# An x ring of seven batches, and one x transfer issued 40 units earlier, in a two-problem attention kernel

## The chip, the cores and the metric

The kernel runs on one core of a Trainium2 chip. The metric is the device time of one execution in microseconds. Before the change the median of four runs is 1052.13 us (lowest 1049.18, highest 1055.1). The profile shown is of one further execution, whose own time is 1052.25 us; its span, from the first to the last profiled instruction, is 1050.5 us.

## The reference

Two independent problems, A and B, of the same shape. Each projects x to queries, attends over a given cache of keys and values, and projects the result; the two outputs are put side by side.

```
# per problem: B, Sq, D = 16, 144, 448;  H, Sk, Dh = 16, 512, 256;  all bfloat16
q = (x @ wq).reshape(B, Sq, H, Dh).transpose(0, 2, 1, 3)
scores = einsum("bhqd,bhkd->bhqk", q, k_cache) * Dh ** -0.5
p = softmax(scores, axis=-1)
o = einsum("bhqk,bhkd->bhqd", p, v_cache)
y = o.transpose(0, 2, 1, 3).reshape(B, Sq, H * Dh) @ wo
# result: concatenate([y_A, y_B], axis=-1), shape (16, 144, 896)
```

## The kernel before, in words

**Units and pairs.** A unit is one head of one batch of one problem: 2 x 16 x 16 = 512 units, numbered U, batch after batch (in the first 32 units two batches are interleaved). Units 0 to 47 take their keys from ordinary loads that TensorE transposes. From unit 48 on (`P0`) keys come from transposing DMAs, and units are handled in pairs, one even and one odd, where their softmax sums are concerned.

**Steps.** A loop over steps i emits the work of several units at different leads. In step i TensorE does the query projection Q of a later unit (L1132), the scores S of unit i+3 (L1163; i+2 before unit 48), the product PV of unit i (L1219), on even steps the row sum SM (L1235), and some matmuls of the output projection (L1335), as many as a rate table allows: one to three pieces of two matmuls in most steps. From unit 48 on most Q instructions do two batches of one head at once and are issued on every other step; for the first and last batches of a problem some do one.

**The softmax path of one unit.** ScalarE takes the exponential of the scores into pt_sb (L1173, two halves). GpSimd adds the four key chunks pairwise: a first add makes pp_sb (L1183), a second add makes one chunk of 128 rows in p2_sb (L1188; the profile writes it p_sb). VectorE adds the lower and upper 64 rows of that (t_halves, L1197, the half-add), into rows 0 to 63 of ps_sb for an even unit and 64 to 127 for an odd one. One matmul with a block matrix of ones then gives the row sums of both units of a pair (L1235). ScalarE makes reciprocals with a logarithm and exponentials (L1243, L1256), and VectorE multiplies PV by them into a ring that the output projection reads (t_evac_ot, L1271). VectorE also casts the queries out of PSUM (L1145 for one batch, L1146 for two) and keeps a running maximum and minimum of the row sums (t_check, L1286), reduced once in a while (L1292), from which one flag is made at the end.

In step i VectorE's program order is: query cast, output multiply of unit i-1, half-add of unit i+2, and on even steps the check of unit i. GpSimd's order is first add, second add, unit after unit.

**Waits.** A small recorder (`_Sched.add`) keeps, for each named buffer, who wrote and who reads it, and turns that into semaphore waits. An engine works in its program order, so an instruction that waits holds all those behind it on that engine. pp_sb and p2_sb have one buffer each, ps_sb has two, pt_sb has four.

**Transfers.** Nearly all DMAs are issued by SP, in one order. A planner makes that order (load_list and the loop behind it): every transfer has a due time (the modelled time of its first use), a step from which its destination is free, and an estimated duration; the planner goes through time, takes what is free soonest and, among these, what is due soonest. No order is made on the chip; SP waits on semaphores in the planned order. The kinds are: v, 512 KB for two units, in a ring of nine slots; k by transposing DMA, 16 units at a time (L1039), in a ring of 32 units; x by transposing DMA (t_load_x, L981 to L991) in a ring xt_sb of six batches, in eight groups; wq and wo, which are loaded for A at the start and again for B near the middle; and the output stores. A group of x that passes the end of the ring, the end of problem A or the end of problem B is split; the last batch of a problem needs three DMAs for its end. A load of x may be issued when the batches that held its slots have had their last query projection.

In what follows, x3 is the group of batches 14 to 17 (14 and 15 of A, 0 and 1 of B), and x4 is the group of batches 18 and 19, which are the third and fourth batch of B.

Of the kernel before, what the change touches and what calls it, by code (L numbers as in the profile page):

```python
# [752 lines left out]
def bass_concat_heads__mha_block_cached__gqa_block_cached__near_ridge_kernel(  # L753
# [23 lines left out]
    Bn, SQ, D = A_x.shape  # L777
    H, SK, DH = A_k_cache.shape[1], A_k_cache.shape[2], A_k_cache.shape[3]
# [3 lines left out]
    NT = NP * NU  # L782
# [4 lines left out]
    NWO = 2 * H  # L787
# [4 lines left out]

    LT = 4
    KW, KR = 16, 32
    NV, NX = 9, 6
    KG = 8
    NNAT = 24
    assert KR % KW == 0 and NU % KW == 0 and KW % KG == 0
# [1 line left out]
    assert X_GROUPS[-1][1] == NP * Bn and H == KW  # L800
    WQ_GROUPS = ((1, 2), (2, 4), (4, 8), (8, 12), (12, 16))
    WARM = 32
    NQT, NPT, NPS, NRI, NOST = 11, 4, 2, 2, 2
    RS = 3
    RC = RS * 128
    XR, X_AT = 48, {0: -4, 1: -2}
# [3 lines left out]

    P0 = NNAT * UV
    NCK = P0 + (NT - P0) // 2
    NRUN = max(n for n in range(1, 33) if NCK % n == 0)
    assert P0 % KG == 0
    HALF_WAVES = (48, 64)
    cuts = {P0} | set(range(P0 // KW * KW + KW, NT, KW)) | set(range(HALF_WAVES[0], HALF_WAVES[1], KG))
# [6 lines left out]
    with contextlib.ExitStack() as es:  # L823
        mem = contextlib.ExitStack()

        def sb(name, shape, dt):
            return mem.enter_context(nc.sbuf_tensor(name, shape, dt))

        def ps(name, shape, dt):
            return mem.enter_context(nc.psum_tensor(name, shape, dt))  # L830
# [8 lines left out]
        pt_sb = sb("pt_sb", [128, NPT, 4, SQ], BF16)  # L839
        ones = sb("ones", [128, 128], BF16)  # L840
        pp_sb = sb("pp_sb", [128, 2, SQ], F32)
        ps_sb = sb("ps_sb", [128, NPS, SQ], BF16)
        rinv_sb = sb("rinv_sb", [128, NRI, SQ], F32)
        p2_sb = sb("p2_sb", [128, SQ], F32)
        ln_sb = sb("ln_sb", [128, SQ], F32)
        run_sb = sb("run_sb", [128, 2, NRUN], BF16)
        runs_sb = sb("runs_sb", [128, 2, NCK // NRUN], F32)
        ost_sb = sb("ost_sb", [128, NOST, D], BF16)
        stat = sb("stat", [128, 4], F32)
        flag_sb = sb("flag_sb", [128, 4], I32)  # L850
        qp_ps = ps("qp_ps", [128, 2, 512], F32)
        s_ps = [ps("s_ps%d" % i, [128, 512], F32) for i in range(3)]
        ot_ps = [ps("ot_ps%d" % i, [128, 512], F32) for i in range(2)]
# [5 lines left out]
        S = _Sched()  # L859
# [19 lines left out]
        def unit(U):  # L879
            if U < 2 * H:  # L880
                return 0, U % 2, U // 2
            pr, r = divmod(U, NU)
            b, h = divmod(r, H)
            return pr, b, h

        def ls(U):

            return 2 if U < P0 else 3

        def lq(U):  # L890
            return ls(U) + 1
# [58 lines left out]
        def t_load_wo(pr, wg):  # L950
            c0 = wg * WOG
            w = wos[pr]

            def e(q):
                return q.dma_start(wo_sb[:, c0:c0 + WOG, :],
                                   w[c0 * 128:(c0 + WOG) * 128, :].rearrange("(c p) n -> p c n", p=128)).then_inc(
                    sems["wo%d" % wg], 16)
            over = [(("xn", g), 1) for g in range(NX) if pr == 0 and wg in x_rows(g)[2]]
            S.add(SP, e, writes=[(("wo", wg), pr)] + over, dma_sem="wo%d" % wg, name="wo%d.%d" % (pr, wg))

        def t_load_x(XG):
# [33 lines left out]

        def x_rows(g):
            n = SQ // XR
            c0 = NWO - (NX - g) * n
            return n, wo_sb[0:XR, c0:c0 + n, :], sorted(set(c // WOG for c in range(c0, c0 + n)))

        def t_load_xn(g):
            n, dst, _wgs = x_rows(g)

            def e(q):
                return q.dma_start(dst, xs[0][g].rearrange("(t p) d -> p t d", p=XR)).then_inc(sems["xn%d" % g], 16)
            S.add(SP, e, writes=[(("xn", g), 0)], dma_sem="xn%d" % g, name="xn%d" % g)
# [145 lines left out]
        def t_s(U):  # L1152
# [16 lines left out]
            for k in range(2):  # L1169
                bank = k if U < P0 else (2 * U + k) % 3  # L1170

                def x(a, k=k, bank=bank):
# [2 lines left out]
                S.add(ACT, x, reads=[(("sp", bank), 2 * U + k)], writes=[(("pt", psl), U)], banks=["s%d" % bank],  # L1175
                      name="ex%d.%d" % (U, k))

        def t_presum(U):
            psl = U % NPT
            sl = U % NPS  # L1180

            def e1(g):
                return g.tensor_tensor(pp_sb[:, :, :], pt_sb[:, psl, 0:2, :], pt_sb[:, psl, 2:4, :], op=ALU.add)  # L1183
            S.add(POOL, e1, reads=[(("pt", psl), U)], writes=[("pp", U)], name="pp%d" % U)
            dst, key = (ps_sb[:, sl, :], (("ps", sl), U)) if U < P0 else (p2_sb[:, :], ("p2", U))

            def e2(g):
                return g.tensor_tensor(dst, pp_sb[:, 0, :], pp_sb[:, 1, :], op=ALU.add)  # L1188
            S.add(POOL, e2, reads=[("pp", U)], writes=[key], name="ps%d" % U)

        def t_halves(U):

            sl = U // 2 % NPS
            p0 = U % 2 * 64

            def e(v):
                return v.tensor_tensor(ps_sb[p0:p0 + 64, sl, :], p2_sb[0:64, :], p2_sb[64:128, :], op=ALU.add)  # L1197

            S.add(DVE, e, reads=[("p2", U)], writes=[(("ps", sl), ("p", U // 2)), ("halves", U)], name="hv%d" % U)

        def ring_cols(pr, b):
            g0 = pr * RP + b * SQ
# [23 lines left out]
        def t_sum(U):  # L1226
            ob = U % 2
            if U < P0:
                rhs, keys = ps_sb[:, U % NPS, :], [("ones", 0), (("ps", U % NPS), U)]
            else:  # L1230
                sl = U // 2 % NPS
                rhs, keys = ps_sb[:, sl, :], [("ones", 1), (("ps", sl), ("p", U // 2))]

            def e(t):
                return t.matmul(ot_ps[ob][:, 2 * SQ:3 * SQ], lhsT=ones[:, :], rhs=rhs, start=True, stop=True)  # L1235
            S.add(PE, e, reads=keys, writes=[(("sum", ob), U)], banks=["ot%d" % ob], name="SM%d" % U)
# [43 lines left out]
        def t_check(U):  # L1280
            ob = U % 2
            n = U if U < P0 else P0 + (U - P0) // 2
            j = n % NRUN
            for k, op in ((0, ALU.max), (1, ALU.min)):
                def e(v, k=k, op=op):
                    return v.tensor_reduce(run_sb[:, k, j:j + 1], ot_ps[ob][:, 2 * SQ:3 * SQ], axis=AX.X, op=op)  # L1286
                S.add(DVE, e, reads=[(("sum", ob), U)], writes=[(("run", k), n // NRUN)], banks=["ot%d" % ob],
                      name="ck%d.%d" % (U, k))
            if j == NRUN - 1:
                for k, op in ((0, ALU.max), (1, ALU.min)):  # L1290
                    def e(v, k=k, op=op):
                        return v.tensor_reduce(runs_sb[:, k, n // NRUN:n // NRUN + 1], run_sb[:, k, :],  # L1292
                                               axis=AX.X, op=op)
# [75 lines left out]
        s_min = -LT  # L1369
# [4 lines left out]
        for r in range(NP * NCH):  # L1374
            pr, rl = divmod(r, NCH)
# [69 lines left out]
        def load_list():  # L1445
            made = []

            def load(use, free, took, fn, *args):
                made.append((at(use) - MARGIN, free, took, fn, args))

            for XG, (g0, g1) in enumerate(X_GROUPS):
                load(first_q[g0], (g1 - NX) * H - lq(NT) if g1 > NX else s_min, 1.3 + 0.55 * (g1 - g0), t_load_x, XG)
            for W, (u0, u1) in enumerate(WAVES):
                last = u1 - 1 - KR
                load(u0 - ls(u0), last - ls(last) + 1 if last >= 0 else s_min, K_FIX + 0.97 * (u1 - u0), t_load_k, W)
            for pr in range(NP):
                for h0, h1 in WQ_GROUPS if pr == 0 else [(h, h + 4) for h in range(0, H, 4)]:
                    load(first_h[pr, h0], NU - H + h1 - lq(NU) if pr else s_min, 0.78 * (h1 - h0), t_load_wq, pr, h0, h1)
                for wg in range(NWG):
                    load(wo_use[pr, wg], wo_done[pr - 1, wg] + 1 if pr else s_min, 1.3, t_load_wo, pr, wg)  # L1460
            for g in X_AT:
                load(X_AT[g], s_min, 0.4, t_load_xn, g)
            for u in range(4):
                load(u - LT, s_min, 0.72, t_load_n, u // 2, u % 2)
            for G in range(2, NNAT):
                load(UV * G - LT, None, 1.44, t_load_n, G)
            for G in range(NT // UV):
                load(UV * G, None, 1.44, t_load_v, G)
# [46 lines left out]
        while i < NT or i in op_at or dma_plan or stores:  # L1515
# [138 lines left out]
```

## Time and profile before

| | |
|---|---|
| median of four runs | 1052.13 us |
| the profiled execution's own time | 1052.25 us |
| its span | 1050.5 us |
| granted TensorE clock, mean | 0.997 |
| TensorE busy | 1031.4 us (98%), 12432 matmuls |
| VectorE busy | 797.1 us (76%) |
| ScalarE busy | 794.0 us (76%) |
| GpSimd busy | 630.7 us (60%) |
| DMA, mean over the span | 280 GB/s |
| first add, L1183 | 512 x 742 ns |
| second add, L1188, from unit 48 on | 464 x 488 ns |
| half-add, L1197 | 464 x 520 ns |
| a k transfer of B, from issue to landing (median) | 25.3 us |
| an x transfer of B, from issue to landing (median) | 5.4 us |

How to read it. The span is cut into the busy time of engines; PE is TensorE's matmuls and PEld its weight loads, DVE is VectorE, ACT ScalarE, POOL GpSimd, SP the engine that issues the transfers. In a row of the page, `out<-in` names the tiles by the kernel's own names with buffer numbers left out; then come the shape, the count, the busy time, the mean of one in ns, the idle time of the engine just before, and what ended it. [...] The DMA share is the sum of the packets' durations over 16 engines and may be over 1, when packets of one engine overlap.

### The profile page before, as it was taken

How to read it: one execution, taken by the hardware profiler on the slowest of the kernel's cores; microseconds unless marked ns; L12 is line 12 of the kernel's file. 1: busy time of each engine (PE TensorE's matmuls, PEld its weight loads, DVE VectorE, ACT ScalarE, POOL GpSimd, SP SyncE). 2: the span in 40 equal slices, each digit the busy share in tenths (PEclk: the TensorE clock that was granted, in tenths of full speed). 3: DMA queues.
4: the chain of work that ended last, by engine and by line, in shares of the span. 5: the costliest groups of instructions: out<-in, count | busy, mean ns of one | idle time of the engine just before them, and what ended most of it. 6: DMA issues, size and time to landing. Idle time of an engine off the chain costs nothing.

```text
span 1050.5 us, 32573 instructions
## 1 busy us (share of the span) xinstructions
PE 1031.4 (98%) x12432; PEld 878.0 (84%) x12432; DVE 797.1 (76%) x2042; ACT 794.0 (76%) x2368; POOL 630.7 (60%) x1030
## 2 busy tenths in 40 slices
PE   8999999999999999999999899999999999999997
PEld 8999888888788888888887688888888888888885
DVE  5776787778777787787686668888787777788774
ACT  5877677778777787878766568787787777788785
POOL 3655556666566666666655456666666666666673
PEclk9999999999999999999999999999999999999999
DMA  9999999999999999999999999999999999999960
GB/s 319 363 331 331 291 263 247 281 283 291 292 297 300 272 278 251 298 278 302 255 299 328 269 291 288 292 272 296 269 265 273 298 281 296 270 282 286 285 226 13
DMA packets 590884, 294.11 MB, mean 280 GB/s; under 512 B 501440, under 2 KB 515904, under 8 KB 590720
## 3 DMA queue, kind: packets, MB, share of 16 engines
q1 hardware_dynamic: 590240, 291.72, 111.5%
q8 instruction: 100, 1.64, 0.6%
q14 instruction: 64, 0.52, 0.2%
q10 hardware_dynamic: 480, 0.23, 0.1%
HBM read 161.74 MB, written 4.13 MB: 158 GB/s over the span
## 4 chain that ended last, share of the span: by engine, by line
PE 89%; DMA 8%; SPq 2%; issue 0%; DVE 0%; ACT 0%; DVEq 0%; ACTq 0%
PE ot_ps L1219 23%; PE s_ps L1163 22%; PE qp_ps L1132 22%; PE op_ps L1335 18%; DMA kt_sb<-in_B_k_cache_dram 2%; DMA kt_sb<-in_A_k_cache_dram 2%; PE ot_ps L1235 2%; DMA wq_sb<-in_A_wq_dram 1%; DMA v_sb<-in_B_v_cache_dram 1%; PE qp_ps L1083 1%; PE s_ps L1083 1%; SPq L1053 1%; DMA wq_sb<-in_B_wq_dram 1%; PE qp_ps L1335 1%; DMA v_sb<-in_A_v_cache_dram 0%; SPq L981 0%
## 5 line engine op out<-in xcount | busy, mean ns | idle before, releaser
L1183 POOL TENSOR_TENSOR pp_sb<-pt_sb 128x288 f32<-128x288 bf16 x512 | 380.0, 742 | 305.8 <-ACT pt_sb L1173 291.2
L1173 ACT ACTIVATE pt_sb<-s_ps 128x288 bf16<-128x288 f32 x1024 | 364.5, 408 | 180.6 <-PE s_ps L1163 174.8
L1163 PE MATMUL s_ps<-qt_sb,kt_sb 128*128 128x144 bf16 x4096 | 340.3, 226 | 5.9 <-DMA kt_sb<-in_B_k_cache_dram 4.9
L1219 PE MATMUL ot_ps<-pt_sb,v_sb 128*128 128x144 bf16 x4096 | 340.2, 226 | 3.5 <-DMA v_sb<-in_B_v_cache_dram 1.9
L1163 PEld LDWEIGHTS s_ps<-qt_sb,kt_sb 128*128 128x128 bf16 x4096 | 288.3, 98 | 54.7 <-issue 5.3
L1256 ACT ACTIVATE rinv_sb<-ln_sb 64x144 f32<-64x144 f32 x928 | 298.2, 321 | 24.2
L1132 PE MATMUL qp_ps<-xt_sb,wq_sb 128*128 128x288 bf16 (+1 forms) x2368 | 300.1, 270 | 2.2 <-DMA wq_sb<-in_B_wq_dram 1.0
L1335 PE MATMUL op_ps<-wo_sb,ring 128*128 128x448 bf16 x1120 | 285.8, 353 | 0.0
L1188 POOL TENSOR_TENSOR p_sb<-pp_sb 128x144 f32<-128x144 f32 x464 | 226.7, 488 | 92.6 <-DVE ps_sb L1197 53.5
L1219 PEld LDWEIGHTS ot_ps<-pt_sb,v_sb 128*128 128x128 bf16 x4096 | 274.2, 98 | 4.6 <-DVE ps_sb L1197 4.1
L1132 PEld LDWEIGHTS qp_ps<-xt_sb,wq_sb 128*128 128x128 bf16 x2368 | 211.8, 98 | 77.0 <-issue 1.6
L1146 DVE CAST qt_sb<-qp_ps 128x576 bf16<-128x576 f32 x216 | 163.3, 756 | 139.1 <-PE qp_ps L1132 138.9
L1197 DVE TENSOR_TENSOR ps_sb<-p_sb 64x144 bf16<-64x144 f32 x464 | 241.4, 520 | 34.7 <-POOL p_sb L1188 15.7
L1271 DVE TENSOR_TENSOR ring<-ot_ps,rinv_sb 128x288 bf16<-128x288 f32 (+2 forms) x640 | 237.4, 387 | 19.1 <-ACT rinv_sb L1256 14.2
L1286 DVE TENSOR_REDUCE run_sb<-ot_ps 128x1 bf16<-128x144 f32 x560 | 144.9, 300 | 42.2 <-ACT rinv_sb L1243 26.3
L1335 PEld LDWEIGHTS op_ps<-wo_sb,ring 128*128 128x128 bf16 x1120 | 94.0, 98 | 20.7 <-issue 0.5
L1243 ACT ACTIVATE ln_sb<-ot_ps 128x144 f32<-128x144 f32 x232 | 67.7, 292 | 34.6 <-PE ot_ps L1235 28.0
L1235 PE MATMUL ot_ps<-ps_sb,ones 128*128 128x144 bf16 x280 | 63.4, 226 | 0.0
L1145 DVE CAST qt_sb<-qp_ps 128x288 bf16<-128x288 f32 x80 | 36.0, 450 | 4.4 <-PE qp_ps L1132 3.6
L1091 ACT ACTIVATE kt_sb<-qp_ps 128x512 bf16<-128x512 bf16 x48 | 29.0, 605 | 1.1 <-PE qp_ps L1083 1.1
L1235 PEld LDWEIGHTS ot_ps<-ps_sb,ones 128*128 128x128 bf16 x280 | 27.4, 98 | 1.1 <-DVE ps_sb L1197 1.1
L1188 POOL TENSOR_TENSOR ps_sb<-pp_sb 128x144 bf16<-128x144 f32 x48 | 23.4, 488 | 6.9 <-PE ot_ps L1235 0.3
(37 smaller groups left out, 163.7 us busy)
## 6 DMA issues: line engine op xcount, KB each, us to landing
v_sb<-in_A_v_cache_dram SPq DMA_DIRECT2D x128, 512.0 KB, 7.4
v_sb<-in_B_v_cache_dram SPq DMA_DIRECT2D x128, 512.0 KB, 7.2
v_sb<-in_A_k_cache_dram SPq DMA_DIRECT2D x22, 512.0 KB, 10.1
out_dram<-ost_sb SPq DMA_DIRECT2D x36, 112.0 KB, 6.4
wo_sb<-in_A_wo_dram SPq DMA_DIRECT2D x8, 448.0 KB, 7.9
wo_sb<-in_B_wo_dram SPq DMA_DIRECT2D x8, 448.0 KB, 8.3
wq_sb<-in_B_wq_dram SPq DMA_DIRECT2D x4, 768.0 KB, 9.4
wq_sb<-in_A_wq_dram SPq DMA_DIRECT2D x3, 768.0 KB, 9.3
```

What stands on the lines that cost most here:

```text
L1132: ins = t.matmul(acc, lhsT=wq_sb[:, kc, c0:c0 + 128], rhs=xt_sb[:, kc, xo:xe + 1:max(xe - xo, 1), :], start=(kc == 0), stop=(kc == 3))
L1146: return v.tensor_copy(qt_sb[:, a:b + 1:b - a, :, :], qp_ps[:, :, 0:2 * SQ].rearrange("p e (u q) -> p u e q", u=2))
L1163: ins = t.matmul(s_ps[bank][:, (c % 2) * SQ:(c % 2 + 1) * SQ], lhsT=kt_sb[:, 2 * c + dc, ko:ko + 128], rhs=qt_sb[:, qsl, dc, :], start=(dc ...
L1173: return a.activation(pt_sb[:, psl, 2 * k:2 * k + 2, :].rearrange("p b q -> p (b q)"), s_ps[bank][:, 0:2 * SQ], AF.Exp, scale=DH ** -0.5)
L1183: return g.tensor_tensor(pp_sb[:, :, :], pt_sb[:, psl, 0:2, :], pt_sb[:, psl, 2:4, :], op=ALU.add)
L1188: return g.tensor_tensor(dst, pp_sb[:, 0, :], pp_sb[:, 1, :], op=ALU.add)
L1197: return v.tensor_tensor(ps_sb[p0:p0 + 64, sl, :], p2_sb[0:64, :], p2_sb[64:128, :], op=ALU.add)
L1219: ins = t.matmul(ot_ps[ob][:, dc * SQ:(dc + 1) * SQ], lhsT=v_sb[:, vsl, j, c * DH + dc * 128:c * DH + (dc + 1) * 128], rhs=pt_sb[:, sl, c, ...
L1256: return a.activation(rinv_sb[p0:p0 + 64, sl, :], ln_sb[h0:h0 + 64, :], AF.Exp, scale=-1.0)
L1271: ins = v.tensor_tensor(ring[:, 2 * h:2 * h + 2, r0:r0 + q1 - q0], ot_ps[ob][:, 0:2 * SQ].rearrange("p (c q) -> p c q", c=2)[:, :, q0:q1], ...
L1286: return v.tensor_reduce(run_sb[:, k, j:j + 1], ot_ps[ob][:, 2 * SQ:3 * SQ], axis=AX.X, op=op)
L1335: ins = t.matmul(acc[0:m, 0:D], lhsT=ring[:, c, col0:col0 + m], rhs=wo_sb[:, c, :], start=(c == op_first), stop=(c == op_last))
```

## The change

The x ring xt_sb goes from six batches to seven (`NX`), and the due time of x4 is set 40 units earlier. The larger ring takes 1152 bytes more of each partition, and these come from other buffers:

- p2_sb is gone; the second add writes over the first half of pp_sb, from which the half-add reads.
- ps_sb has one buffer in place of two. Before unit 48 the odd units use a part of the second output staging buffer instead.
- The run of row-sum reductions is 20 long in place of 28, so there are 14 runs in place of 10, kept in bfloat16, and the flag shares a tile with other small values.
- The two batches of x that are loaded in natural order at the start lie in the last six columns of wo_sb in place of earlier ones.

With seven slots the places where x groups pass the ring's end are others (multiples of seven), and so are the splits of the groups and the pairs of batches whose order is turned in a double query projection. The order of instructions on TensorE, ScalarE and GpSimd is the same as before; on VectorE only the reductions of runs stand elsewhere. On SP's queue x3 and x4 stand earlier, x3 ahead of the k transfer for units 192 to 207 and x4 ahead of that for units 224 to 239, and three v transfers stand one place earlier, ahead of a k transfer each.

```diff
-    NV, NX = 9, 6
+    NV, NX = 9, 7
...
-    NQT, NPT, NPS, NRI, NOST = 11, 4, 2, 2, 2
+    NQT, NPT, NRI, NOST = 11, 4, 2, 2
...
-    NRUN = max(n for n in range(1, 33) if NCK % n == 0)
+    NRUN = max(n for n in range(1, 21) if NCK % n == 0)
...
-        ps_sb = sb("ps_sb", [128, NPS, SQ], BF16)
+        ps_sb = sb("ps_sb", [128, SQ], BF16)
         rinv_sb = sb("rinv_sb", [128, NRI, SQ], F32)
-        p2_sb = sb("p2_sb", [128, SQ], F32)
...
-        runs_sb = sb("runs_sb", [128, 2, NCK // NRUN], F32)
+        runs_sb = sb("runs_sb", [128, 2, NCK // NRUN], BF16)
         ost_sb = sb("ost_sb", [128, NOST, D], BF16)
-        stat = sb("stat", [128, 4], F32)
-        flag_sb = sb("flag_sb", [128, 4], I32)
+        stat = sb("stat", [128, 8], F32)
+        flag_sb = stat.bitcast(I32)[:, 4:8]
...
-            c0 = NWO - (NX - g) * n
+            c0 = NWO - (len(X_AT) - g) * n
...
+        def ps_natural(U):
+            if U % 2:
+                return ost_sb[:, 1, 0:SQ], (("ost", 1), ("ps", U))
+            return ps_sb[:, :], ("ps", U)
...
-            dst, key = (ps_sb[:, sl, :], (("ps", sl), U)) if U < P0 else (p2_sb[:, :], ("p2", U))
+            dst, key = ps_natural(U) if U < P0 else (pp_sb[:, 0, :], ("pp", ("p2", U)))
...
-                return v.tensor_tensor(ps_sb[p0:p0 + 64, sl, :], p2_sb[0:64, :], p2_sb[64:128, :], op=ALU.add)
-
-            S.add(DVE, e, reads=[("p2", U)], writes=[(("ps", sl), ("p", U // 2)), ("halves", U)], name="hv%d" % U)
+                return v.tensor_tensor(ps_sb[p0:p0 + 64, :], pp_sb[0:64, 0, :], pp_sb[64:128, 0, :], op=ALU.add)
+
+            S.add(DVE, e, reads=[("pp", ("p2", U))], writes=[("ps", ("p", U // 2)), ("halves", U)], name="hv%d" % U)
...
-                load(first_q[g0], (g1 - NX) * H - lq(NT) if g1 > NX else s_min, 1.3 + 0.55 * (g1 - g0), t_load_x, XG)
+                load(first_q[g0] - (40 if g0 == Bn + 2 else 0), (g1 - NX) * H - lq(NT) if g1 > NX else s_min, 1.3 + 0.55 * (g1 - g0), t_load_x, XG)
```

More of the change, by code (lines that the diff above doesn't have):

```diff
@@ L957, in e @@
                     sems["wo%d" % wg], 16)
-            over = [(("xn", g), 1) for g in range(NX) if pr == 0 and wg in x_rows(g)[2]]
+            over = [(("xn", g), 1) for g in X_AT if pr == 0 and wg in x_rows(g)[2]]
             S.add(SP, e, writes=[(("wo", wg), pr)] + over, dma_sem="wo%d" % wg, name="wo%d.%d" % (pr, wg))
@@ L1176, in t_s @@
                       name="ex%d.%d" % (U, k))
+        def ps_natural(U):
+            if U % 2:
+                return ost_sb[:, 1, 0:SQ], (("ost", 1), ("ps", U))
+            return ps_sb[:, :], ("ps", U)
         def t_presum(U):
             psl = U % NPT
-            sl = U % NPS
             def e1(g):
@@ L1191, in t_halves @@
         def t_halves(U):
-            sl = U // 2 % NPS
             p0 = U % 2 * 64
             def e(v):
-                return v.tensor_tensor(ps_sb[p0:p0 + 64, sl, :], p2_sb[0:64, :], p2_sb[64:128, :], op=ALU.add)
-            S.add(DVE, e, reads=[("p2", U)], writes=[(("ps", sl), ("p", U // 2)), ("halves", U)], name="hv%d" % U)
+                return v.tensor_tensor(ps_sb[p0:p0 + 64, :], pp_sb[0:64, 0, :], pp_sb[64:128, 0, :], op=ALU.add)
+            S.add(DVE, e, reads=[("pp", ("p2", U))], writes=[("ps", ("p", U // 2)), ("halves", U)], name="hv%d" % U)
         def ring_cols(pr, b):
@@ L1228, in t_sum @@
             if U < P0:
-                rhs, keys = ps_sb[:, U % NPS, :], [("ones", 0), (("ps", U % NPS), U)]
-            else:
-                sl = U // 2 % NPS
-                rhs, keys = ps_sb[:, sl, :], [("ones", 1), (("ps", sl), ("p", U // 2))]
+                rhs, key = ps_natural(U)
+                keys = [("ones", 0), key]
+            else:
+                rhs, keys = ps_sb[:, :], [("ones", 1), ("ps", ("p", U // 2))]
             def e(t):
```

## The prediction

> **What bounds the kernel now.** I read the page first: TensorE is busy 98% of the span, so a gain can only come out of its waits, and a loss must make a new one. Then the list of waits for TensorE alone (engine, tile and line, what it waited for: us in total, times, longest):
>
> ```profile
> PE s_ps L1163 <- DMA kt_sb<-in_B_k_cache_dram: 4.9, 1, 4.9
> PE ot_ps L1219 <- DMA v_sb<-in_B_v_cache_dram: 1.9, 2, 1.2
> PE ot_ps L1219 <- DMA v_sb<-in_A_v_cache_dram: 1.4, 1, 1.4
> ```
>
> The large waits are for transfers, none for VectorE or GpSimd. TensorE's timeline puts three of problem B's at 523.25 (0.96, wq), 563.28 (1.20, v) and 603.76 (4.89, k). Then the table by windows (us, busy time and count of PE, PEld, DVE, ACT, POOL; granted clock, DMA share, GB/s), around the x transfer that SP issued at 463.04, and around the longest wait:
>
> ```profile
> 460.00:467.00 7.00, 7.00 (x81) 5.80 (x79) 5.98 (x18) 5.00 (x16) 4.13 (x8) 1.00 1.05 392
> 468.00:470.00 2.00, 2.00 (x32) 1.85 (x30) 1.97 (x6) 1.76 (x7) 1.26 (x3) 1.00 1.39 74
> 471.00:472.50 1.50, 1.50 (x23) 1.40 (x22) 0.87 (x3) 0.94 (x3) 0.99 (x2) 1.00 1.14 36
> 600.00:620.00 20.00, 16.24 (x166) 13.27 (x167) 10.38 (x28) 10.39 (x31) 7.44 (x13) 0.91 1.19 297
> ```
>
> The DMA engines are a second bound: in windows of 20 us their share is over 1 from 20 to 1000 us, at some 390 GB/s on v and 290 on transposes, and each change of kind leaves a hole: 2 us at 74 GB/s before the x data, 1.5 us at 36 behind it. The last line adds a clock of 0.91 after the long wait: 0.09 x 20 = 1.8 us more lost.
>
> The diff also takes buffers away on the GpSimd-VectorE path, so I read that path in one pair of units, GpSimd's timeline, then VectorE's (start, duration, engine and line, idle before it):
>
> ```profile
> 699.62 0.73 POOL L1183 TENSOR_TENSOR pp_sb<-pt_sb 128x288 f32<-128x288 bf16 x1
> 700.59 0.49 POOL L1188 TENSOR_TENSOR p_sb<-pp_sb 128x144 f32<-128x144 f32 x1 [0.24 <-DVE ps_sb L1197]
> 701.22 0.78 POOL L1183 TENSOR_TENSOR pp_sb<-pt_sb 128x288 f32<-128x288 bf16 x1
> ```
>
> ```profile
> 701.11 0.30 DVE L1197 TENSOR_TENSOR ps_sb<-p_sb 64x144 bf16<-64x144 f32 x1
> 701.40 0.52 DVE L1286 TENSOR_REDUCE run_sb<-ot_ps 128x1 bf16<-128x144 f32 x2
> 702.38 0.76 DVE L1146 CAST qt_sb<-qp_ps 128x576 bf16<-128x576 f32 x1 [0.46 <-PE qp_ps L1132]
> 703.05 0.45 DVE L1271 TENSOR_TENSOR ring<-ot_ps,rinv_sb 128x288 bf16<-128x288 f32 x1
> 703.53 0.78 DVE L1197 TENSOR_TENSOR ps_sb<-p_sb 64x144 bf16<-64x144 f32 x1
> ```
>
> GpSimd's first add of the next unit (0.73) runs beside VectorE's half-add, and its second add waits for that. A half-add takes 0.30 with GpSimd idle, 0.78 beside its first add.
>
> **The change part by part: the new wait.** With p2_sb folded into pp_sb, the first add of unit U+1 waits for the half-add of U; before, only the second add did. Behind it on GpSimd stand only the second add and the next units; VectorE's next half-add waits for these, and behind that in VectorE's order stand the check (L1286), the q eviction (L1146) and the output eviction (L1271), for which S and PV of the following units wait. The loop from half-add to half-add: handoff 0.08 (699.74+0.77=700.51 to 700.59), first add 0.73, gap 0.14 (701.22+0.78 to the second add at 702.15, rounded down), second add 0.49, handoff 0.03, half-add.
>
> [...] Its mean in the page is 520 ns, its list by line reads 302/306/847 (least, median, most). [...] By the mean the loop is 0.08+0.73+0.14+0.49+0.03+0.52=1.99 us a unit. [...] every half-add costs 0.30: 1.77 us. [...] I take 1.77. It also frees VectorE of about 0.47 us a pair, which no TensorE wait needs.
>
> Most pairs hold one double q eviction. From the odd unit's half-add: 0.30, then 0.08+0.73+0.14+0.49+0.03 and the even half-add 0.30 (2.07), the check 0.52 from 0.01 before its end (2.58), the q eviction 0.76 (3.34), the output eviction 0.45 from 0.09 before that ends (3.70), 0.03, the next odd half-add: 3.73 us a pair. TensorE's row sums at 700.75 and 704.55 stand 3.80 apart, and over 620 to 1000 its 1568 score matmuls, 8 a unit, give 3.88 on average. So the wait hides, with 0.07 to spare in the tightest pairs and 0.15 on average. Where several tight pairs follow, or the q evictions are shorter and so faster paced, I let the trace's starts slip by the loop: 0.3 to 0.8 us of lateness near 382, 437, 460, 500 and 570, which the DMA waits at 523 to 604 swallow (7.05 us together), and 0.4 us in all near 720 and 973, on the path (bounds 0 and 0.8).
>
> The cover is gone in the last units. Two row sums one pair apart in TensorE's timeline:
>
> ```profile
> 1021.73 0.23 PE L1235 MATMUL ot_ps<-ps_sb,ones 128*128 128x144 bf16 x1
> 1021.79 0.54 PE L1335 MATMUL op_ps<-wo_sb,ring 128*128 128x448 bf16 x2
> ...
> 1025.05 0.23 PE L1235 MATMUL ot_ps<-ps_sb,ones 128*128 128x144 bf16 x1
> ```
>
> 3.32 us a pair there, against 2 x 1.77 = 3.54: 0.22 lost in each of the last 8 pairs, 1.76, less about 0.25 of margin that is used up first: +1.5 (bounds 0.5 and 2.5).
>
> The single ps_sb makes the even half-add wait for the row sum of the pair before: that ends at 700.75+0.23=700.98, the half-add starts at 701.11 now and 0.2 later after: nothing. Below unit 48 the odd unit's slot is ost_sb's second, which no output chunk uses so early: nothing. Four more pairs of run reductions (176 ns each, 1.4 us in all), a zeroing of 64x504 for 64x432 (418 ns, some 0.07 more) and the packed flag lie in VectorE's idle quarter: nothing; with no cover the reductions cost 1.4.
>
> **The change part by part: the transfers.** On SP's queue only this moves: x4 (second problem's batches 3 and 4; issue 3.96 at 463.04) goes ahead of the k transfer of 433.45; x3 (four DMAs at 400.39, 5.6) ahead of the k transfer of 370.53; and the v transfers for units 204, 220 and 252 go each ahead of the k transfer they followed. Splits of x at ring ends change (15 x DMAs before and after): x1 and x5 in two, x2 whole, x7 three for four.
>
> The two k transfers behind x start up to 5.6 and 4.0 later. They land at 391.50 and 455.30 and are first used at 403.99 and 465.23: 12.5 and 9.9 us to spare, so no wait. The k transfers of 406.06 and 467.06 can be issued 2.8 and 2.6 sooner, but issuing is not moving: v data queued before 463 still flows at 390 GB/s till 467.5. The same bytes and as many changes of kind lie before 604 in another order. What is really won is the hole around the four x DMAs at 401 to 409 (share 0.29, 1 GB/s from 404 to 406), which now falls under a v backlog. Nothing won is one bound; the other is x4's whole passage, 467.5 to 472.5, off the queue before 604: 4.5 of the 4.89 us and the 1.8 of the clock with it. I take 1.2, near the low end, since the share leaves little idle DMA time to win: -1.2. The v transfer behind x5 lands 1.4 us before its use; the split may cost it 0 to 0.5: +0.2.
>
> **Sum**, on the profiled execution (1052.25: span 1050.5 and 1.75 around it): 1052.25 + 1.5 + 0.4 + 0.2 - 1.2 = 1053.15. The median shown is 0.12 lower, so 1053.0.
>
> **The rivals.** (a) *The x transfer was hidden anyway and what it wins, the loop gives back* (my forecast): x4 lands 91 us ahead of its first use. 1053.0.
> (b) *Faster: x4's passage comes off the DMA-bound stretch whole.* For it: from 515.9 on SP issues to 604 without waiting for an engine, each transfer late by the one before it. Against: the DMA engines are as full where x4 goes. 1052.1 - 4.5 - 1.8 + 2.1 = 1047.9; with the waits at 523 and 563 gone as well, 1045.7. [...] The trace has this one wait to go by; I keep the 1.8.
> (c) *Slower: the half-add loop becomes the bound everywhere.* Place: handoff to the first add and VectorE's order behind it. It decides once a pair's loop is 0.15 longer than my 3.73. At 0.2 longer: 0.05 on 105 pairs from 604 on is 5.3, the last 8 pairs 1.6 more; earlier ones are swallowed: 1053.0 + 6.9 = 1059.9. For it: only 0.07 to spare in tight pairs, and a handoff read from a few rows. Against: every term is a repeated row.
> (d) *Slower: a k or v transfer pushed back by x misses its use*: 2 to 5 us, 1057.
>
> **How the numbers follow.** Chances: (a) 0.57, (b) 0.17, (c) 0.18, (d) 0.08. The runs before spread over 1049.18 to 1055.1, so 0.5% (5.3 us, below 1046.9 or above 1057.4) is about what a measurement can tell from no change. Faster by that needs (b) with the earlier waits gone too: 0.12. Slower: (c) and part of (d), with some of (a)'s spread: 0.28. Within: 0.60. The range holds (a), most of (b) and (c): 1046.5 to 1061.
>
> **What would show it.** Right: half-adds nearly all near 0.30; first adds released by the half-add instead of the exponential; row sums about 3.54 apart at the end, with TensorE waiting on the half-add there and nowhere for long; the wait near 604 still over 3 us. Wrong on (b) if that wait is under 1 us; wrong on (c) if row sums stand over 3.9 apart between 620 and 1000; wrong on (d) if a transfer of k before 500 us has a wait behind it.

## The result and the profile after

| | before | after |
|---|---|---|
| median of the runs | 1051.6 us (63 runs) | 1057.47 us (42 runs) |
| ratio, 95% interval | | 1.0048, [1.0038, 1.0059] |
| the profiled execution's own time | 1052.25 us | 1056.6 us |
| its span | 1050.5 us | 1054.8 us |
| VectorE busy | 797.1 us | 706.0 us |

The change costs 5.1 us (0.0048 x 1051.6; 4.0 to 6.2). The forecast, 1053.0, stood for a cost of 0.9. The measured time lies inside the range of 1046.5 to 1061, at the edge of the 0.5% that was called no change.

The page's rows of after for the first add, the second add and the half-add:

```profile
L1186 POOL TENSOR_TENSOR pp_sb<-pt_sb 128x288 f32<-128x288 bf16 x512 | 373.0, 729 | 374.8 <-DVE ps_sb L1199 246.1
L1191 POOL TENSOR_TENSOR pp_sb<-pp_sb 128x144 f32<-128x144 f32 x464 | 226.7, 489 | 36.4
L1199 DVE TENSOR_TENSOR ps_sb<-pp_sb 64x144 bf16<-64x144 f32 x464 | 141.2, 304 | 158.1 <-POOL pp_sb L1191 128.9
```

The half-add fell from 520 to 304 ns, and the first add now waits for it: 246.1 us of GpSimd's idle time are released by VectorE. That much is as forecast, and it costs nothing by itself. What costs is read from TensorE. Its list of waits in after:

```profile
PE s_ps L1162 <- DMA kt_sb<-in_B_k_cache_dram: 4.5, 1, 4.5
PE ot_ps L1221 <- DMA v_sb<-in_A_v_cache_dram: 3.9, 1, 3.9
PE s_ps L1082 <- DMA v_sb<-in_A_k_cache_dram: 1.7, 4, 0.7
PE ot_ps L1221 <- DMA v_sb<-in_B_v_cache_dram: 1.2, 1, 1.2
```

The long k wait near 604 is still there (4.9 before), and the v wait that was 1.4 is 3.9. TensorE's timeline puts them in place:

```profile
269.76 0.91 PE L1221 MATMUL ot_ps<-pt_sb,v_sb 128*128 128x144 bf16 x8 [3.91 <-DMA v_sb<-in_A_v_cache_dram]
503.13 0.67 PE L1162 MATMUL s_ps<-qt_sb,kt_sb 128*128 128x144 bf16 x8 [0.51 <-DVE qt_sb L1144]
606.54 1.12 PE L1162 MATMUL s_ps<-qt_sb,kt_sb 128*128 128x144 bf16 x8 [4.55 <-DMA kt_sb<-in_B_k_cache_dram]
```

The middle row is new: before the change no matmul between 425 and 510 us waited for VectorE. The table by windows of after (us, busy time and count of PE, PEld, DVE, ACT, POOL; granted clock, DMA share, GB/s):

```profile
260.00:280.00 20.00, 16.09 (x168) 12.87 (x166) 9.41 (x25) 10.72 (x33) 9.19 (x16) 0.91 1.08 321
...
600.00:620.00 20.00, 15.45 (x147) 11.98 (x145) 8.16 (x22) 9.11 (x27) 7.38 (x13) 0.83 1.17 307
```

Before, the clock was 1.00 in the first and 0.91 in the second. Half clock for 3.41 us is 1.7 us lost and takes 0.09 off a window of 20 us. Ahead of the last units before has one stretch of this length, from 603.50; after has one, from 270.02, and one of 6.83 us, from 604.52.

And the last units, row sums of two pairs, then GpSimd and VectorE beside them:

```profile
1028.55 0.23 PE L1237 MATMUL ot_ps<-ps_sb,ones 128*128 128x144 bf16 x1
1032.17 0.23 PE L1237 MATMUL ot_ps<-ps_sb,ones 128*128 128x144 bf16 x1
```

```profile
1026.83 0.73 POOL L1186 TENSOR_TENSOR pp_sb<-pt_sb 128x288 f32<-128x288 bf16 x1 [0.55 <-ACT pt_sb L1172]
1027.64 0.49 POOL L1191 TENSOR_TENSOR pp_sb<-pp_sb 128x144 f32<-128x144 f32 x1
1028.61 0.73 POOL L1186 TENSOR_TENSOR pp_sb<-pt_sb 128x288 f32<-128x288 bf16 x1 [0.48 <-DVE ps_sb L1199]
1029.41 0.49 POOL L1191 TENSOR_TENSOR pp_sb<-pp_sb 128x144 f32<-128x144 f32 x1
```

```profile
1026.39 0.30 DVE L1199 TENSOR_TENSOR ps_sb<-pp_sb 64x144 bf16<-64x144 f32 x1 [1.05 <-PE s_ps L1162]
...
1028.16 0.31 DVE L1199 TENSOR_TENSOR ps_sb<-pp_sb 64x144 bf16<-64x144 f32 x1 [0.31 <-POOL pp_sb L1191]
...
1030.01 0.30 DVE L1199 TENSOR_TENSOR ps_sb<-pp_sb 64x144 bf16<-64x144 f32 x1 [1.05 <-PE s_ps L1162]
```

A pair takes 3.62 us where it took 3.32. The three engines' rows show one closed loop: half-add, first add, second add, half-add. From an even half-add to the odd one it takes 1.77 us. Back again it takes 1.85: the second add ends at 1029.90, and the even half-add starts 0.11 later; the odd one starts 0.03 after its second add (1028.13 to 1028.16). The even one has two semaphores to wait for since the half-sums have one buffer: GpSimd's, for the second add, and TensorE's, for the row sum of the pair before. That row sum was done at 1028.78, so the TensorE named in the row was not what it waited for; the second wait is there all the same. All half-adds of this trace for which VectorE stood idle show it: from the end of the second add to their start, the even ones take 104 ns (median of 122, 102 to 105) and the odd ones 34 ns (125, 33 to 35). On TensorE the delay shows at the weight loads: between 1005 and 1038 us those of L1162 stand idle for 3.7 us for the q cast (L1144), which is queued on VectorE behind the half-add.

**Where the time went, unit by unit.** I take the time between two row sums, subtract TensorE's DMA waits in between, and subtract the same of before. Units 494 to 508: 23.23 us before, 25.37 after, no DMA wait in either: +2.14 (0.31 a pair over 7 pairs). Units 200 to 240, where query casts are single: 427.14 to 500.55 before, 429.92 to 504.14 after, again no DMA wait: +0.81. Units 300 to 494: -0.6, nothing lost. TensorE's DMA waits over the whole trace sum to 12.7 us against 11.8: +0.9. (In it are +2.5 near 269 and -0.8 in the three waits from 523 to 606, 6.23 after and 7.05 before.) At half clock TensorE worked for 3.15 us before (603.76 to 606.9), and for 3.4 and 4.8 us after, which loses half of each: 4.1 against 1.6, +2.5. This makes +5.7, and the rest, -1.4, lies ahead of unit 180. The two profiled executions differ by 4.35.

### The profile page after: what moved, and what is told of

Its sections match the earlier page's. It is cut to its first block, busy times and chain, and to the rows that moved or that the text cites. A ratio compares the mean times of both kernels' runs of the same rounds, so it can differ in the third digit from the quotient of the medians.

```text
span 1054.8 us, 32350 instructions
## 1 busy us (share of the span) xinstructions
PE 1033.3 (98%) x12432; PEld 877.7 (83%) x12432; DVE 706.0 (67%) x2050; ACT 794.2 (75%) x2368; POOL 623.9 (59%) x1030
## 4 chain that ended last, share of the span: by engine, by line
PE 88%; DMA 5%; POOL 2%; SPq 1%; ACT 1%; DVE 1%; issue 1%; POOLq 0%; DVEq 0%; ACTq 0%
PE qp_ps L1131 22%; PE ot_ps L1221 22%; PE s_ps L1162 22%; PE op_ps L1337 18%; DMA kt_sb<-in_B_k_cache_dram 2%; PE ot_ps L1237 2%; DMA wq_sb<-in_A_wq_dram 1%; POOL pp_sb L1186 1%; PE qp_ps L1082 1%; PE s_ps L1082 1%; POOL pp_sb L1191 1%; DMA wq_sb<-in_B_wq_dram 1%; PE qp_ps L1337 1%; SPq L1052 1%; DMA v_sb<-in_B_v_cache_dram 1%
## 5 line engine op out<-in xcount | busy, mean ns | idle before, releaser
L1186 POOL TENSOR_TENSOR pp_sb<-pt_sb 128x288 f32<-128x288 bf16 x512 | 373.0, 729 | 374.8 <-DVE ps_sb L1199 246.1
L1162 PE MATMUL s_ps<-qt_sb,kt_sb 128*128 128x144 bf16 x4096 | 340.5, 226 | 6.5 <-DMA kt_sb<-in_B_k_cache_dram 4.5
L1162 PEld LDWEIGHTS s_ps<-qt_sb,kt_sb 128*128 128x128 bf16 x4096 | 287.7, 98 | 57.7 <-DVE qt_sb L1144 5.5
L1191 POOL TENSOR_TENSOR pp_sb<-pp_sb 128x144 f32<-128x144 f32 x464 | 226.7, 489 | 36.4
L1199 DVE TENSOR_TENSOR ps_sb<-pp_sb 64x144 bf16<-64x144 f32 x464 | 141.2, 304 | 158.1 <-POOL pp_sb L1191 128.9
L1237 PE MATMUL ot_ps<-ps_sb,ones 128*128 128x144 bf16 x256 | 58.0, 226 | 0.0
L1144 DVE CAST qt_sb<-qp_ps 128x288 bf16<-128x288 f32 x80 | 35.9, 449 | 6.7 <-PE qp_ps L1131 6.0
L1237 PEld LDWEIGHTS ot_ps<-ps_sb,ones 128*128 128x128 bf16 x256 | 25.1, 98 | 0.0
L1090 DVE COPY kt_sb<-s_ps 128x512 bf16<-128x512 bf16 x48 | 20.0, 416 | 3.1 <-PE s_ps L1082 2.7
```

The source lines that it names most:

```text
L1162: ins = t.matmul(s_ps[bank][:, (c % 2) * SQ:(c % 2 + 1) * SQ], lhsT=kt_sb[:, 2 * c + dc, ko:ko + 128], rhs=qt_sb[:, qsl, dc, :], start=(dc ...
L1199: return v.tensor_tensor(ps_sb[p0:p0 + 64, :], pp_sb[0:64, 0, :], pp_sb[64:128, 0, :], op=ALU.add)
```

## The experiments

Each kernel was timed beside the kernel before on the same chip: experiments 1 to 4 on one chip, 5 to 8 on a second, 9 to 12 on a third. The chip of the changed kernel's own 42 runs is not on record. The expectations of the first eight were written with several theories at hand: the loop at the end, the x transfers, longer DMA waits. The last four name three: S, the shared place makes the DMA waits longer; R, the single half-sum buffer does; M, the rest is the moved x transfers or scatter.

**1. The buffers alone.** The changed kernel with the ring and all transfers as before.

```diff
-    NV, NX = 9, 7
+    NV, NX = 9, 6
...
-                load(first_q[g0] - (40 if g0 == Bn + 2 else 0), ...
+                load(first_q[g0], ...
```

> The changed buffers alone (second add over pp_sb, one ps_sb, short reduction runs), with the ring of six and SP's order as before. Theory T (the loop of first add, second add and half-add costs time only in the last units, where the changed kernel's row sums stand 0.31 us a pair later than before over 7 pairs; the rest of its loss comes with the moved x transfers): 2.2 us over before. Rival B (the buffers cost all, also by way of longer waits for DMA at 269 and 606 us): 5 us over before. Rival N (the buffers cost nothing): within 1 us of before.

Measured: 1054.0 us, ratio 1.0034 [1.001, 1.0058]. The trace shows +2.15 in the last units, +0.82 in units 200 to 240. The k wait near 604 is 6.53, the v wait near 268 is absent. The cost of 3.6 us (1.0 to 6.1) lies between theory T's 2.2 and rival B's 5. By the medians most of the cost stands with no x transfer moved.

**2. Ring of seven, x transfers in their old places.** The free point is computed as for six.

```diff
-                load(first_q[g0] - (40 if g0 == Bn + 2 else 0), (g1 - NX) * H - lq(NT) if g1 > NX else s_min, ...
+                load(first_q[g0], (g1 - 6) * H - lq(NT) if g1 > 6 else s_min, ...
```

> The changed kernel with its ring of seven, but x3 and x4 on SP's queue where they stood before. Theory T (the moved x3 and x4 cost what the last units do not): 2.2 us over before. Rival B (buffers): 5 us over before, as the changed kernel. Rival S (the splits of x at other ring ends): more than the kernel with changed buffers alone.

Measured: 1053.35 us, 1.0035 [1.0022, 1.0047], and the same two losses (2.15, 0.81). The longer ring with its other splits costs nothing beside experiment 1 that these intervals could show.

**3. A place of its own for the second add in the last units.** The changed kernel, with the second add's output of units 464 to 511 in two ring slots of x that nothing uses by then.

```diff
+        def p2_place(U):
+            if U >= 464:
+                own = xt_sb[:, 0, 4:6, :].rearrange("p b q -> p (b q)").bitcast(F32)
+                return own, ...
+            return pp_sb[:, 0, :], ...
```

> The changed kernel, but from unit 464 on the second add writes to a place of its own in two x slots that are free by then, so the first add no longer waits for the half-add there. Theory T: row sums in the last units 3.32 us apart again, 2.2 us less than the changed kernel, so about 2.9 over before. Rival (the lateness of the end comes from elsewhere, such as the single ps_sb, which stays): no less than the changed kernel.

Measured: 1054.27 us, 1.0039 [1.0026, 1.0052]. Row sums of this kernel in TensorE's timeline:

```profile
1027.15 0.23 PE L1250 MATMUL ot_ps<-ps_sb,ones 128*128 128x144 bf16 x1
1030.47 0.23 PE L1250 MATMUL ot_ps<-ps_sb,ones 128*128 128x144 bf16 x1
```

3.32 a pair, as before: the loss of the last units is gone (0.00 from unit 494 to 508), so the shared place makes it. The total fell by less than the 2.2 hoped for: it is 4.1 over before (2.7 to 5.5; theory T named 2.9), and the execution profiled waited 3.69 near 268, 5.93 near 604 and 1.67 near 730.

**4. The transfer of x4 cut to 16 of 288 rows,** on the kernel before. It leaves out most of the data of two batches.

```diff
+                        if XG == 4:
+                            rows = 16
-                        ins = q.dma_start_transpose(dst, src).then_inc(sems[sem], 16)
+                        ins = q.dma_start_transpose(dst[:, :, 0:rows], src).then_inc(sems[sem], 16)
```

> The kernel before, but x4 loads 16 rows in place of 288, so that its passage is all but gone from the queue; the scores of those two batches of problem B are computed on what the slots held, and this part of the output is left wrong. Rival b of the prediction (x4's passage stands in a DMA-bound stretch and moves the wait near 604 one for one): wait near 604 under 1 us, 4 to 6 us under before. The prediction's own reading (little is to be won there): 0 to 1.2 us under before, wait near 604 still over 3.5 us.

Measured: 1049.52 us, 0.9993 [0.9983, 1.0003]. Its list of waits:

```profile
PE s_ps L1165 <- DMA kt_sb<-in_B_k_cache_dram: 6.2, 1, 6.2
```

With nearly all of x4 gone the wait near 604 is 6.2, not shorter. The whole passage is worth 0.7 us by the median and 1.8 at most.

**5. The 40 units alone taken back.**

```diff
-                load(first_q[g0] - (40 if g0 == Bn + 2 else 0), ...
+                load(first_q[g0], ...
```

> The changed kernel without the 40 units: x4's due time as before, the ring of seven kept. The recorded order of all five engines and their waits are the changed kernel's, since it is the earlier free slot that moves x3 and x4. Theory T (last units 2.2, the order of x3 and x4 the rest): the changed kernel's own ratio again, 1.0048, and a mean granted clock near 0.994. If instead the rest of its loss was the chip or the day: 1.0025 to 1.0035, as the kernel with the ring of seven and the old order, and a clock near 0.996.

Measured: 1056.3 us, 1.0056 [1.0038, 1.0074]. The programs of all five engines are those of the changed kernel, in order and in waits: with seven slots the earlier free point alone moves x3 and x4. This is a second measurement of the changed kernel, and its interval holds the first one's ratio, 1.0048.

**6. Experiment 1 with the second add's own place in the last units.** The two edits above together, with ring slots 2 and 3.

> The changed buffers with the ring of six and SP's order as before, and from unit 464 on a place of its own for the second add's output (two free x slots). Theory T (the buffers cost in the last units alone): row sums at the end 3.32 us a pair, and the time of before within 1 us. Rival B (the buffers also cost elsewhere): 1.3 us or more over before.

Measured: 1055.53 us, 1.0049 [1.0031, 1.0067], loss in the last units 0.00, in units 200 to 240 0.84. Its wait near 268:

```profile
PE ot_ps L1234 <- DMA v_sb<-in_A_v_cache_dram: 3.0, 1, 3.0
```

The theory that the buffers cost in the last units only is refuted. Up to unit 464 this kernel and that of experiment 1 run the same programs, and yet one waits 3.0 near 268 and the other not at all. A single profile can't say whether a kernel has that wait. Nor is the clock the same: its mean is 0.9942 over the six runs here and 0.9961 over the eight of experiment 1, on the other chip, where the kernel before had 0.9961 and 0.9959.

**7. x3 moved, x4 in its old place.**

```diff
+                xring = NX if XG == 3 else 6
-                load(first_q[g0] - (40 if g0 == Bn + 2 else 0), (g1 - NX) * H - lq(NT) if g1 > NX else s_min, ...
+                load(first_q[g0], (g1 - xring) * H - lq(NT) if g1 > xring else s_min, ...
```

> The changed kernel with only x3 ahead of its k transfer; x4 stands where it stood before. Theory T with x4 as what costs: the ratio of the ring of seven in the old order, 1.0035. With x3 as what costs: the changed kernel's, 1.0048. Both apart by about the width of one interval.

Measured: 1056.46 us, 1.0052 [1.0032, 1.0072]: no different from experiment 5, where x4 is moved too, nor from experiment 2 beyond the intervals.

**8. The loads of wo for B behind the k transfer they preceded,** on the kernel before. It tests what the queue ahead of the long wait is worth. Its output projection of B starts 16 units later.

```diff
-    OP_DELAY, OP_START, OP_RATE = 2, (28, 16), ((200, 1.04), (240, 0.85), (292, 1.4), (600, 1.1))
+    OP_DELAY, OP_START, OP_RATE = 2, (28, 32), ((200, 1.04), (240, 0.85), (292, 1.4), (600, 1.1))
```

> The kernel before, with the second problem's output projection started 32 units into it in place of 16, so that its eight wo loads (448 KB each, some 1.15 us at 390 GB/s) stand behind the k transfer of 577 us. If the wait near 604 comes of what is queued ahead of that k transfer (the DMA engines are full there): the wait is gone with its half-clock window, 4.9 + 1.7, so 4 to 6.6 us under before. If the wait comes of the k transfer's own duration: wait near 604 still over 3 us and no gain.

Measured: 1066.34 us, 1.0159 [1.0137, 1.018]. TensorE's timeline:

```profile
590.69 0.66 PE L1163 MATMUL s_ps<-qt_sb,kt_sb 128*128 128x144 bf16 x8 [3.29 <-DMA kt_sb<-in_B_k_cache_dram]
637.72 1.11 PE L1163 MATMUL s_ps<-qt_sb,kt_sb 128*128 128x144 bf16 x8 [13.65 <-DMA kt_sb<-in_B_k_cache_dram]
```

The k transfer is issued at 562.82 in place of 577.48, and its wait is 3.29. The next one, now behind wo, v and x, goes out at 614.12 in place of 604.92 and makes 13.65. Moving bytes in this stretch moved the wait. Of the two sides of the expectation the second came nearer: the first wait is still over 3 us and nothing is gained. Neither foresaw the longer wait behind it. The later output projection also changes TensorE's own order, so the 16 us need not be the transfers' alone.

**9 to 12. One buffer at a time,** on the kernel before, with its ring and transfers. The third joins the edits of the first two.

```diff
# 9: fold in the last units only; 10: fold without them (U < 464)
+        def p2_place(U):
+            if U >= 464:
+                return pp_sb[:, 0, :], ("pp", ("p2", U))
+            return p2_sb[:, :], ("p2", U)
# 11: one half-sum buffer
-        ps_sb = sb("ps_sb", [128, NPS, SQ], BF16)
+        ps_sb = sb("ps_sb", [128, SQ], BF16)
# 12: 10 and 11
```

Experiment 9: 

> The kernel before, with the second add's output put over the first place of the first add's buffer for units 464 to 511 only; single half-sum buffer, ring and transfers stay as before. All theories: the first add of the last 16 units waits for the half-add, 0.31 us a pair, row sums 2.15 us later at the end; ratio 1.0020, and no longer DMA waits.

Experiment 10: 

> The kernel before, with the second add's output put over the first place of the first add's buffer for units 48 to 463, and the place of its own kept for 464 to 511, so that the last units pair as before. Theory S (the shared place itself makes the DMA waits longer): ratio 1.0025 to 1.003, a wait over 3 us near 268. Theory R (the single half-sum buffer does) and theory M (the remainder is the moved x transfers or scatter between executions): 0.9995 to 1.0005.

Experiment 11: 

> The kernel before, with one half-sum buffer in the place of two (odd units of the first three batches keep theirs in the second output buffer, as in the changed kernel); the second add keeps its own place. Theory R: ratio 1.0025 to 1.003, a wait over 3 us near 268. Theories S and M: 0.9995 to 1.0005.

Experiment 12: 

> Both of the two buffer changes at once up to unit 463, last units as before, ring and transfers as before. Theories S and R: ratio 1.0025 to 1.003 as the one of the two alone; if neither alone costs but both together do, the cost is one of the lost slack between the adds and the row sums. Theory M: 0.9995 to 1.0005, and the +1.0049 seen with the same buffers on another chip is then not a cost of the buffers alone.

Measured, with the losses outside the DMA waits worked out as above, and the granted clock averaged over all runs of the kernel (0.9961 for the kernel before beside them):

| | ratio, interval | units 200-240 | units 494-508 | mean clock |
|---|---|---|---|---|
| 9, fold, last units only | 1.0023 [1.0013, 1.0032] | 0.00 us | 1.58 us | 0.9960 |
| 10, fold, without them | 1.0007 [0.9995, 1.0019] | 0.63 | 0.00 | 0.9949 |
| 11, one half-sum buffer | 1.0022 [1.0013, 1.0031] | 0.43 | 0.00 | 0.9956 |
| 12, 10 and 11 | 1.0034 [1.0015, 1.0053] | 0.85 | 0.00 | 0.9953 |
| after | 1.0048 [1.0038, 1.0059] | 0.81 | 2.14 | 0.9942 |

Row sums of experiment 9, where the half-sums still have two buffers:

```profile
1022.38 0.23 PE L1242 MATMUL ot_ps<-ps_sb,ones 128*128 128x144 bf16 x1
1025.93 0.23 PE L1242 MATMUL ot_ps<-ps_sb,ones 128*128 128x144 bf16 x1
```

3.55 a pair, where the changed kernel has 3.62 (its expectation, 0.31 lost a pair, is missed: 0.23). Its GpSimd and its VectorE show the handoff to an even half-add, which has one semaphore to wait for here:

```profile
1026.80 0.49 POOL L1193 TENSOR_TENSOR pp_sb<-pp_sb 128x144 f32<-128x144 f32 x1
```

```profile
1027.32 0.30 DVE L1204 TENSOR_TENSOR ps_sb<-pp_sb 64x144 bf16<-64x144 f32 x1 [0.98 <-POOL pp_sb L1193]
```

From the end at 1027.29 to 1027.32 are 0.03 us, where the changed kernel takes 0.11. With one half-sum buffer (experiments 11 and 12) the median of such even handoffs is 103 ns, with two (9 and 10) 33. The parts add up: 0.0023 + 0.0007 + 0.0022 = 0.0052, beside 0.0048 for the whole. But the intervals leave some 0.002, or 2 us, for the x transfers to cost or to win, and pairs of one chip do not settle it. On the first chip experiment 3 (transfers moved, last units repaired) stands 0.0004 above experiment 2 (neither), though the repair is worth 0.0020 in the trace: a cost of 0.0024, give or take 0.0018. On the second, experiment 5 (moved, not repaired) stands 0.0007 above experiment 6 (repaired, not moved): a gain of 0.0013, give or take 0.0025. Theory M falls for experiments 11 and 12: the half-sum buffer costs without any transfer moved. The size that theory R named (0.0025 to 0.003) is just above the median of experiment 11, and the sign it named, a wait over 3 us near 268, is absent: experiments 9 and 11 have none there, 10 has 0.38 and 12 has 1.03. Theory S is not borne out at its size, 0.0025 and more.

In the fold without the last units the mean clock is lower by 0.0012. On 1050 us that is 1.3 us, which more than covers its 0.7. In the single half-sum buffer the clock explains 0.5 of 2.3 us and the tight pairs near 500 us another 0.43 at most, if no DMA wait swallows it. The other 1.4 us I could not find in its one profile. The reductions of runs, the bfloat16 maxima and the packed flag were not run by themselves; experiment 6 has them and experiment 12 has not, and their intervals overlap, on different chips.

## Why the prediction was right or wrong

**The loop: right, and sized too small.** The half-add at 0.30 and the loop of 1.77 us a unit came out as charged, not as the mean of before would have them (0.52 and 1.99): 302, 304 and 307 ns are the least, median and largest of the 464 half-adds. The trace of before shows what goes with its two sizes. The 219 half-adds that start while GpSimd is in an add take 553 to 847 ns, and each ends 162 to 169 ns after that add; the 245 others take 302 to 307 ns. In after every half-add waits for the second add and every first add for the half-add, and none of the 464 half-adds overlaps an add of GpSimd. What holds a half-add back beside an add is not shown. (The prediction's list of waits left out 1.1 us for GpSimd at the start, which the sum does not need. Two terms of the loop were off and cancel: the handoff to the first add is 0.14, not 0.08, the gap behind it 0.08, not 0.14.) The +1.5 of the fold is what experiment 9 measured: 1.58, of 7 pairs at 0.226. What failed is the step "the single ps_sb makes the even half-add wait for the row sum of the pair before: nothing". The row sum was done in time, as the step said. But the handoff with a second semaphore to wait for took 0.07 us more (104 against 34 ns), and in the last units, where the loop is closed, it comes on top: 0.31 a pair. So the term of +1.5 measured 2.14. Experiment 3 shows that the shared place makes the loss, experiment 9 what the second half-sum buffer was worth in it.

**The tight pairs: another place than charged, and swallowed as said.** I charged 0.4 near 720 and 973 and nothing near 437 to 500, since the waits at 523 to 604 would swallow it. Units 300 to 494 lost nothing. Units 200 to 240 lost 0.81, of which 0.63 between 500.5 and 504.1, and in this trace the waits did swallow it: the three from 523 to 606 are 0.82 shorter together. At the row sum of unit 200 TensorE is 2.78 us behind the trace of before and at that of unit 300 3.60, of which 0.83 is the longer half clock at 606. What those waits did not swallow is the 2.78, which comes mostly from the wait near 269 and the half clock behind it. The timelines of TensorE and SP show why, before and then after:

```profile
493.24 0.66 PE L1163 MATMUL s_ps<-qt_sb,kt_sb 128*128 128x144 bf16 x8
493.94 21.93 SPq L1039 DMA_TRANSPOSE kt_sb<-in_B_k_cache_dram  x1
...
577.48 22.76 SPq L1039 DMA_TRANSPOSE kt_sb<-in_B_k_cache_dram  x1
```

```profile
496.19 0.66 PE L1162 MATMUL s_ps<-qt_sb,kt_sb 128*128 128x144 bf16 x8
496.89 21.74 SPq L1038 DMA_TRANSPOSE kt_sb<-in_B_k_cache_dram  x1
...
580.18 22.78 SPq L1038 DMA_TRANSPOSE kt_sb<-in_B_k_cache_dram  x1
```

The TensorE row is the scores of unit 239, the last that read the slots which the k transfer of units 256 to 271 overwrites. SP issues that transfer 0.03 us behind their end, so it is as late as TensorE: 2.95. The k transfer that TensorE waits for near 604 is the one at 577.48 (units 288 to 303). It waits for no semaphore; its slots had been free since 562.08, 15.4 us before. It is issued 2.70 later and lands 2.8 later in after because it stands behind the other one in SP's single order. So the DMA wait swallowed what delay of TensorE came after the last place where the queue ahead of that transfer waited for TensorE, here 493.9 as far as the trace shows, and passed on what came before. I hold this for these two traces: in ten of the other kernels that landing is between 0.8 us sooner and 1.3 later than TensorE's lateness at unit 200 would have it.

**The transfers: -1.2, not there.** The wait near 604 went from 4.89 to 4.55 in the profiles and is 4.5 to 6.5 in all kernels with that queue. Cutting x4 is worth 0.7 (at most 1.8), and moving x3 and x4 shows no gain (experiment 2 against 5 and 7, on different chips; within one chip the effect is open by some 2 us). The hole around the x DMAs is filled in after: from 400 to 410 us the DMA share is 1.05 at 387 GB/s, where before had 0.79 and 173. But over 370 to 604 us the share is 1.17 in both, at 285 GB/s after and 283 before, so over the stretch the filled hole shows almost nothing. Where it went is not shown. The +0.2 for the v transfer behind x5 isn't seen in after, where it lands 2.6 us before its use; in experiment 7, with the same split of x5, TensorE waited 1.10 us for it (at 640.89).

**No term for the clock.** The sum held one stretch of half clock fixed. After has a mean clock of 0.9942 over its runs, the kernel before 0.996: 0.0018 x 1055 = 1.9 us at most (part of a stretch can fall into the wait itself, as 2.0 us did near 604 in after, from 604.52 to 606.54), about one stretch of 3.41 us more in each run. What makes them is not shown, and the fold alone does not: experiments 1 and 2 have it and a mean clock of 0.9961. Programs that are the same up to unit 464 had 0.9961 on one chip and 0.9942 on another (experiments 1 and 6), and one of them has the long wait near 268 in its profile and the other not.

**The rivals.** (b) is wrong, by the wait near 604 and by experiment 4. (c) named 1059.9 and stands nearer to the time than the forecast, but its mechanism is wrong: from unit 310 to 490 the row sums are 3.88 us apart in after and 3.89 before. (d) named 1057, and is wrong too: the k transfers behind x3 and x4 land 7.0 and 7.8 us before their use. What the sum lacked is 0.6 in the last units, the 1.2 not won and up to 1.9 for the clock, less the 0.4 charged near 720 and 973 and the 0.2 not seen: 3.1 of the 4.2 us between +0.9 and +5.1. The other 1.1 stays open; it is no more than the uncertainty of the measured cost (4.0 to 6.2), and experiment 11 has 1.4 us that were not placed either. The range of 1046.5 to 1061 took in (c) as well, so that the time fell into it is owed to its width and says little for the mechanism.

None of the kernels is faster than the kernel before.

## What to carry to other kernels

When two buffers on one path are made one each, close the loop again with all the new waits together, in the stretch where the consumer is fastest: a wait that is long fulfilled cost nothing here at 3.88 us a pair (units 310 to 490), and its handoff, 0.07 us a pair, where a pair took 3.32 before. In these two traces a DMA wait hid TensorE's delay (0.81 us in units 200 to 240, mostly behind 500.5) where it came after the last point at which that transfer, or one ahead of it in the same queue, waited for TensorE (493.9), and passed on the one that came before (2.95 us late there, 2.70 at the issue); look up what frees the destinations along the queue. Before counting a gain from moving a transfer inside a DMA-bound stretch, cut that transfer and see what it is worth at all (x4's 5 us of passage were worth 0.7).

## What the hardware showed that was not expected

In experiment 6 TensorE stopped at about 265.4 us and went on at 268.45 after a wait of 3.03 us. Its table by windows (us, busy time and count of PE; granted clock, DMA share, GB/s):

```profile
266.00:268.00 2.00, 0.00 (x0) 0.89 1.00 322
268.00:270.00 2.00, 1.55 (x11) 0.50 1.03 390
270.00:272.00 2.00, 2.00 (x10) 0.50 1.06 405
272.00:274.00 2.00, 2.00 (x18) 0.50 1.06 388
274.00:276.00 2.00, 2.00 (x25) 0.90 1.05 384
```

The clock fell within the wait (0.89: half clock for the last 0.44 us of that window), some 2.1 us after the stop, and stayed at half for 6.8 us; for the last 5.9 of them TensorE was working again. In after the wait was longer, 3.91 us, and the half clock shorter, 3.41 us; it began at 270.02, 0.26 us after TensorE had gone on. From 3 us up a longer wait for a DMA did not cost more clock:

| wait of TensorE | its length | half clock | lost in it |
|---|---|---|---|
| before, at 268.29 | 1.43 us | none | 0 |
| experiment 6, at 268.45 | 3.03 | 6.8 us | 3.0 us |
| after, at 269.76 | 3.91 | 3.41 | 1.7 |
| after, at 606.54 | 4.55 | 6.83 | 2.4 |
| before, at 603.76 | 4.89 | 3.41 | 1.6 |

The last column is half of the time that TensorE worked at half clock. What decides when a stretch begins and how long it lasts is not shown in these traces. The prediction kept its 1.8 us of clock on the one wait near 604; of these five the length does not tell what is lost.
